# Turning a small accumulation around on TensorE: 32-column tiles with v stationary in place of phi(k) stationary

## The chip, the cores and the metric

The kernel runs on one core of one Trainium2 chip. The metric is the device time of one execution in microseconds (us). Three runs of the kernel before gave 148.71, 149.34 and 149.08 us, so the median is 149.08 us.

## The reference, cut to what matters

One transformer layer with a linear attention and a dense block side by side, over 2048 rows of 448 numbers, 16 heads of 28:

```python
xn  = layernorm(x)                              # 2048 x 448
q, k, v = split_heads(xn @ wqkv)                # 16 heads of 28
pq, pk  = q @ w_phi[h], k @ w_phi[h]
phi_q = concat(softmax(pq), softmax(-pq))       # 56 features per head
phi_k = concat(softmax(pk), softmax(-pk))
kv  = phi_k^T @ v                               # per head 56 x 28, summed over all 2048 rows
z   = sum over rows of phi_k                    # per head 56
num = phi_q @ kv ;  den = phi_q @ z + 1e-6
out = x + merge_heads(num / den) @ wo + silu(xn @ w1) @ w2
```

The change is about `kv` and `z`. All heads together they are 16 small products of 56 x 2048 by 2048 x 29, where a column of ones beside the 28 columns of v gives z.

## The kernel before, in words

The 2048 rows are 16 tiles of 128, in 4 chunks of 4. A tile t of phi(k) lies in `E[:, t % 6, 1, :]`: 128 rows, 16 heads of 64 columns each, 56 used and 8 of zeros. The matching v lies in `vb` as 16 x 29 columns.

Every matmul of the kernel uses half of TensorE's rows. Two matmuls stand side by side, one on partitions 0 to 63 and one on 64 to 127 (`pair`, `tpair`, L437 and L450), and write two different PSUM banks. All stationary operands have 128 columns.

The units of work on TensorE are these. `F1(c, i)` is a block of 14 matmuls of 512 columns for the dense layer's hidden activations of chunk c. `QK(t)` and `V(t)` are 14 matmuls of 448 columns for one tile's q and k, and for v of two tiles. `F2_early(t)` and, for the late tiles, `F2_ph` are 28 matmuls of 448 columns for the dense layer's second product. `KV(t)` adds one tile to `kv`. `U(t)` multiplies phi(q) of two tiles by `kv`. `WO` is the output projection.

`KV(t)` (L731) takes two heads at a time. The stationary operand is a 64-row half of phi(k) with 128 columns (two heads), the moving operand the 58 columns of v of the same two heads. Half of the 128 x 58 result is a product of one head with the other and is never read. That is 8 pairs, 16 matmuls per tile, 256 in the whole. The sums of the two halves of the rows stand in PSUM banks 6 and 7.

`KVZ_fin` (L738) ends the sum: for each of two partition ranges, ScalarE copies bank 6 to `KVt` and VectorE adds bank 7 and writes `KVZ`, in which `U` finds kv with the 56 features on the partitions.

Around this, the order of TensorE's work is the order in which the program text issues it. Everything else is placed by a planner (`_Prog.schedule`) that walks the operations with assumed durations and due times; it fixes the order on ScalarE, VectorE, GpSimd and the DMA queue, and semaphores are set from the data dependencies. In chunk 1 and chunk 2, four `KV` stand one by one between `F1` blocks. In chunk 3, two `KV` follow `V(12)` and two follow `QK(15)`, and the last four stand between the `F1` blocks. So the 16 `KV` are 14 places on TensorE: 12 of one tile and 2 of two tiles. After the last `KV` come `F1(3, 5)`, then `KVZ_fin`'s result is used by `U(0)`, which stands after the first pair of `F1(3, 6)`; `U(8)` stands inside the first half of the late `F2` of tiles 8 and 9, after its fourth step (ft = 3); then `U(2)`.

Of the kernel before, what the change touches and what calls it, by code (L numbers as in the profile page):

```python
# [7 lines left out]
F32 = mybir.dt.float32  # L8
ACTF = mybir.ActivationFunctionType
# [320 lines left out]
def bass_parallel_sum__linear_kernel_hedgehog__dense_activation_silu__prompt_kernel(  # L330
# [10 lines left out]
    S, D, H, DH, FF = 2048, 448, 16, 28, 1792  # L341
    NT = S // 128
# [3 lines left out]
    NCH = S // 512  # L346
# [5 lines left out]
    with es:  # L352
        def sb(name, shape, dt):
            return es.enter_context(nc.sbuf_tensor(name, shape, dt))

        NE, NV, NX, NXC, NYE, NH = 6, 3, 4, 3, 8, 3
# [9 lines left out]
        E = sb("E", [128, NE, 2, 1024], BF16)  # L366
        vb = sb("vb", [128, NV, 2, H * (DH + 1)], BF16)
        xnd = sb("xnd", [128, NX, NS * 128], BF16)
        Ye = sb("Ye", [128, NYE, D], F32)
        KVZ = sb("KVZ", [128, 8, DH + 1], BF16)  # L370
        KVt = sb("KVt", [128, 8, DH + 1], F32)
        BD = sb("BD", [128, NB, 2 * DH], BF16)
        ident = sb("ident", [128, 128], BF16)
        neghalf = sb("neghalf", [128, 1], F32)
# [28 lines left out]
        def bank(b):  # L403
            return psum[:, b * 512:(b + 1) * 512]

        def bank16(b):
            return psum16[:, b * 1024:(b + 1) * 1024]
# [11 lines left out]
        P = _Prog()  # L419
# [14 lines left out]
        def d_dve(n, mode=1):  # L434
            return n * 1.042 / mode + 158.0

        def pair(mms, n, name, dur=None):  # L437
            reads = []
            writes = []
            for (dst, lhsT, rhs, st, sp) in mms:  # L440
                reads += [lhsT, rhs]
                writes.append(dst)

            def fn(e):
                for (dst, lhsT, rhs, st, sp) in mms:
                    ins = e.matmul(dst, lhsT, rhs, start=st, stop=sp, skip_group_check=True)  # L446
                return ins
            return P.op("pe", dur if dur else max(n / 2.4 + 2.5, 27.0), fn, reads=reads, writes=writes, name=name)

        def tpair(trs, n, name):  # L450
            reads = []
            writes = []
            for (dst, src, idn) in trs:
                reads += [src, idn]
                writes.append(dst)

            def fn(e):
                for (dst, src, idn) in trs:
                    ins = e.transpose(dst, src, idn)  # L459
                return ins  # L460
            return P.op("pe", max(n / 2.4 + 2.5, 29.0), fn, reads=reads, writes=writes, name=name)

        def act(dst, src, func, n, table=None, scale=1.0, name="", reads=None, writes=None):
            return P.op("act", d_act(n), lambda e: e.activation(dst, src, func, scale=scale),  # L464
                        reads=reads or [src], writes=writes or [dst], table=table, name=name)

        def dve(fn, dur, reads, writes, name):
            return P.op("dve", dur, fn, reads=reads, writes=writes, name=name)
# [12 lines left out]
        HALF = (LO, HI)  # L481
# [199 lines left out]
        def F1(c, i, mid=None):  # L681
            P.unit = f"F1_{c}_{i}"
            sl = take()
            for s in range(NS):
                pair([(bank(2 * sl + q)[:, 0:512], w1_sb[HALF[q], s, i * 128:(i + 1) * 128],
                       xw(q, c, s, 0, 512), s == 0, s == NS - 1) for q in range(2)], 512, "f1")
                if mid is not None and s == 0:
                    mid()
            F1silu(sl, i, c, 0, 512)
# [40 lines left out]

        def KV(t):  # L731
            P.unit = f"KV{t}"
            for c in range(8):
                pair([(bank(6 + q)[:, c * 58:(c + 1) * 58], E[HALF[q], t % NE, 1, c * 128:(c + 1) * 128],
                       vb[HALF[q], (t // 2) % NV, t % 2, c * 58:(c + 1) * 58], t == 0 and c == 0, t == NT - 1)
                      for q in range(2)], 58, "kv")

        def KVZ_fin():  # L738
            P.unit = "KVZ"
            for q, (p0, p1) in enumerate(((0, 56), (64, 120))):  # L740
                v = [bank(6 + b)[p0:p1, 0:464].rearrange("p (c n) -> p c n", n=58)[:, :, q * 29:(q + 1) * 29] for b in range(2)]
                tmp = KVt[p0:p1]
                act(tmp, v[0], ACTF.Identity, 232, name="kvz_a")
                dst = KVZ[p0:p1]
                dve(lambda e, dst=dst, a=v[1], tmp=tmp: e.tensor_tensor(dst, a, tmp, ALU.add), d_dve(232), [v[1], tmp], [dst], "kvz_d")

        def F2(t, mid=None, at=7):
            c, j = divmod(t, 4)
# [22 lines left out]
            for q in range(2):  # L771
                act(bk[q], xs[q], ACTF.Identity, b - a, name="seed")

        def F2_ph(t, sl, ph, a, b, mid=None, at=3):
            c, j = divmod(t, 4)
            for ft in range(FT):
                P.unit = f"F2_{t + ph}"
                mms = []
                for q in range(2):
                    h = q ^ ph  # L780
                    mms.append((bank(2 * sl + h)[:, a:b], hT[HALF[q], c % NH, ft, (j + h) * 128:(j + h + 1) * 128],
                                w2_sb[HALF[q], ft, a:b], False, False))
                swapped(pair(mms, b - a, "f2"), (2 * sl, 2 * sl + 1), ph)
                if mid is not None and ft == at:
                    mid()

        uc = [0]

        def U(t, sl=3):
            P.unit = f"U{t}"  # L790
            for i, tt in enumerate((t, t + 1)):
                for c in range(8):
                    o0 = i * 232 + c * 29
                    pair([(bank(2 * sl + q)[:, o0:o0 + 29], phT[q * 64:q * 64 + 56, tt, c, :], KVZ[q * 64:q * 64 + 56, c, :], i == 0 and c == 0, True)
                          for q in range(2)], 29, "u", dur=25.0)
            ub = uc[0] % NO
            uc[0] += 1
            Uv = two(sl)[:, :, 0:464].rearrange("p b (c n) -> p b c n", n=29)
            dn = den[:, ub, :].rearrange("p (b c) -> p b c", b=2)
            dve(lambda e: e.tensor_scalar(dn, Uv[:, :, :, DH], EPS_DEN, None, ALU.add), 200, [Uv], [den[:, ub, :]], "den")  # L800
            dve(lambda e: e.reciprocal(rden[:, ub, :], den[:, ub, :]), 360, [den[:, ub, :]], [rden[:, ub, :]], "rden")
            for i in range(2):
                for q in range(2):
                    src = bank(2 * sl + q)[:, i * 232:(i + 1) * 232].rearrange("p (c n) -> p c n", n=29)[:, :, 0:DH]
                    src = src.rearrange("p c (s e) -> p c s e", e=4)
                    r = rden[:, ub, q * 16 + i * 8:q * 16 + (i + 1) * 8]
                    rb = r[:, :, None, None].broadcast_to([128, 8, NS, 4])
                    dst = o_pr[:, ub].rearrange("p (s n) -> p s n", s=NS)[:, :, i * 64:(i + 1) * 64].rearrange("p s (c r e) -> p c r s e", r=2, e=4)[:, :, q]
                    dve(lambda e, dst=dst, src=src, rb=rb: e.tensor_tensor(dst, src, rb, ALU.mult), d_dve(224),  # L809
                        [src, r], [dst], "o")  # L810
            P.dma(lambda e: e.dma_start_transpose(out=oT[:, ub], in_=o_pr[:, ub]), 0, reads=[o_pr[:, ub]],
                  writes=[oT[:, ub]], name="oT_dma", issue=1250.0, fixed=3100.0)
            return ub
# [227 lines left out]

        ub = {}

        def first_u():
            ub[EPAIRS[0]] = U(EPAIRS[0])

        LATE = list(range(8, 16))
        EPAIRS = [0, 2, 4, 6]
        for c in range(NCH):
            if c == NCH - 1:  # L1050
                phase_e(c, F2E[c])
            if c > 0:
                for i in range(FH):
                    F1(c, i, first_u if c == NCH - 1 and i == 6 else None)
                    if i in ((3, 4, 5, 6) if c == 1 else (1, 2, 4, 5) if c == 2 else (1, 2, 3, 4)):
                        kv(1)
                    if c == NCH - 1 and i == 4:
                        KVZ_fin()
            if c < NCH - 1:
                phase_e(c, F2E[c])  # L1060
                if c < NCH - 2:
                    for t in range(4 * c + 8, 4 * c + 12):
                        prep(t)
        def nextu(t, sl=3):
            if sl is None:
                sl = take()
                give(sl)
            ub[t] = U(t, sl)

        sls = {}  # L1070

        def ph0(l, a, b, mid=None):
            sls[l, a] = take()
            seed(l, sls[l, a], a, b)
            F2_ph(l, sls[l, a], 0, a, b, mid)
# [7 lines left out]
            WO_two(l, ub[l], sls[l, 0], 0, D)  # L1083

        M = D // 2
        ph0(8, 0, D, lambda: nextu(8, None))
        nextu(2)
        ph1(8, 0, D)
        ph0(10, 0, D)
# [123 lines left out]
```

## Time and profile before

| | us |
|---|---|
| median of three runs | 149.08 |
| the profiled execution, whole | 148.71 |
| its span (first to last instruction) | 147.0 |
| TensorE matmuls busy | 142.4 (97%) |
| TensorE weight loads busy | 87.8 (60%) |
| VectorE busy | 92.3 (63%) |
| ScalarE busy | 89.0 (61%) |
| GpSimd busy | 76.3 (52%) |

The granted TensorE clock is full from the second of the 40 slices of the span on. A matmul's end is modelled, so the busy times of matmuls that lie side by side overlap; what a unit costs TensorE is read from the time between its first start and the first start of what follows. The difference of 1.7 us between the whole and the span lies outside the profile.

### The profile page before, as it was taken

The page shows a single profiled execution, that of the slowest core. Times are in us where ns is not written, and L with a number is a line of the kernel's source. Part 1 is how long each engine was busy: PE and PEld are TensorE (multiplying, and loading weights), DVE is VectorE, ACT ScalarE, POOL GpSimd, SP SyncE. Part 2 cuts the span into 40 slices and gives each one's busy share as a digit, 9 for nine tenths or more (in the row PEclk, how much of TensorE's full clock was granted, in tenths as well). Part 3 has the DMA queues.
Part 4 walks back from the last instruction along what each step waited for, and adds up shares of the span by engine and source line. Part 5 has one row for each costly group of instructions (what it writes and reads, how often), then busy time and mean ns, then how long its engine had stood idle before and what let it go on. Part 6 is the DMA issues. An engine that isn't in the chain of part 4 may idle for free.

```text
span 147.0 us, 5049 instructions
## 1 busy us (share of the span) xinstructions
PE 142.4 (97%) x2188; PEld 87.8 (60%) x2188; DVE 92.3 (63%) x176; ACT 89.0 (61%) x119; POOL 76.3 (52%) x87
## 2 busy tenths in 40 slices
PE   6999999999999999999999999999999999999992
PEld 2589975555556555555555556655555555557871
DVE  1977469999977496840167997871067254466632
ACT  4248789997767784975987767598593023040401
POOL 3335025059999959899122999999980000000000
PEclk9999999999999999999999999999999999999999
DMA  5997989985930895359870049333663505315473
GB/s 142 389 253 159 329 250 256 78 166 157 164 78 4 159 181 123 90 131 151 173 158 0 0 101 46 71 76 74 85 134 71 121 4 179 75 60 131 127 129 125
DMA packets 44110, 19.11 MB, mean 130 GB/s; under 512 B 37240, under 2 KB 43448, under 8 KB 44088
## 3 DMA queue, kind: packets, MB, share of 16 engines
q1 hardware_dynamic: 43432, 17.87, 57.9%
q10 hardware_dynamic: 656, 0.92, 1.7%
q8 instruction: 17, 0.28, 0.9%
q14 instruction: 5, 0.04, 0.1%
HBM read 8.17 MB, written 1.84 MB: 68 GB/s over the span
## 4 chain that ended last, share of the span: by engine, by line
PE 93%; DMA 3%; DVE 1%; POOL 0%; issue 0%; ACT 0%; SPq 0%; POOLq 0%
PE psum L446 92%; DMA E<-E 3%; PE psum L459 1%; DVE E L809 1%; POOL hT L485 0%; DVE x_sb L843 0%; ACT xT L464 0%; POOL neghalf L484 0%; SPq L1153 0%; POOLq L1198 0%
## 5 line engine op out<-in xcount | busy, mean ns | idle before, releaser
L713 POOL TENSOR_TENSOR E<-E,Rk 128x896 bf16<-128x896 bf16 x32 | 53.3, 1700 | 7.0 <-DVE Rk L708 5.3
L446 PE MATMUL psum<-xT,w_sb 64*128 64x512 bf16 (+2 forms) x522 | 46.8, 324 | 0.3 <-ACT xT L464 0.3
L446 PE MATMUL psum<-w_sb,hT 64*128 64x448 bf16 (+1 forms) x504 | 45.3, 328 | 0.0
L446 PEld LDWEIGHTS psum<-w_sb,hT 64*128 64x128 bf16 x504 | 25.7, 94 | 16.4 <-ACT psum L464 0.2
L706 DVE TENSOR_REDUCE Sk<-E 128x64 f32<-128x1792 bf16 x16 | 31.9, 2004 | 2.9 <-ACT E L464 2.9
L446 PEld LDWEIGHTS psum<-xT,w_sb 64*128 64x128 bf16 x522 | 25.1, 94 | 13.9 <-issue 0.4
L464 ACT ACTIVATE hT<-psum 128x1024 bf16<-128x1024 f32 (+1 forms) x29 | 28.1, 993 | 8.8 <-PE psum L446 8.5
L464 ACT ACTIVATE E<-psum 128x896 bf16<-128x896 f32 x32 | 27.4, 917 | 6.4 <-PE psum L446 5.2
L446 PE MATMUL psum<-wqk,xT 64*128 64x448 bf16 x224 | 23.7, 349 | 0.0
L446 PEld LDWEIGHTS psum<-wqk,xT 64*128 64x128 bf16 x224 | 12.2, 94 | 8.6
L464 ACT ACTIVATE psum<-x_sb 128x448 f32<-128x448 bf16 (+1 forms) x10 | 4.6, 470 | 20.0 <-PE psum L446 19.4
L581 POOL TENSOR_TENSOR rstd<-ve,neghalf 128x1 f32<-128x1 f32 x16 | 9.1, 571 | 7.2 <-DVE ve L579 6.4
L765 POOL TENSOR_TENSOR Ye<-Ye,x_sb 128x448 f32<-128x448 f32 x8 | 8.2, 1037 | 8.8 <-DVE Ye L763 8.8
L446 PE MATMUL psum<-wo_sb,E 64*128 64x448 bf16 (+1 forms) x126 | 11.9, 328 | 0.1
L446 PE MATMUL psum<-wv_sb,xT 64*128 64x448 bf16 x112 | 12.0, 349 | 0.0
L589 DVE TENSOR_SCALAR xnd<-x_sb,mv,rstd 128x896 bf16<-128x896 bf16 x12 | 8.3, 723 | 5.9 <-POOL rstd L581 5.9
L573 DVE BATCH_NORM_STATS2 st<-x_sb 128x6 f32<-128x448 bf16 x16 | 9.5, 605 | 3.3 <-DMA x_sb<-in_A_x_dram 3.3
L763 DVE TENSOR_TENSOR Ye<-psum,Ye 128x448 f32<-128x448 f32 x8 | 5.0, 622 | 10.3 <-ACT Ye L464 10.2
L833 DVE TENSOR_TENSOR x_sb<-psum,Ye 128x448 bf16<-128x448 f32 x8 | 4.8, 607 | 9.7 <-PE psum L446 6.8
L809 DVE TENSOR_TENSOR E<-psum,rden 128x224 bf16<-128x224 f32 x32 | 10.2, 383 | 0.2
L446 PEld LDWEIGHTS psum<-wv_sb,xT 64*128 64x128 bf16 x112 | 5.9, 94 | 4.0
L446 PEld LDWEIGHTS psum<-wo_sb,E 64*128 64x128 bf16 x126 | 5.8, 94 | 4.0 <-DMA E<-E 0.4
(48 smaller groups left out, 100.0 us busy)
## 6 DMA issues: line engine op xcount, KB each, us to landing
w_sb<-in_B_w_dram SPq DMA_DIRECT2D x4, 448.0 KB, 5.8
out_dram<-x_sb SPq DMA_DIRECT2D x7, 224.0 KB, 2.1
w_sb<-in_B_w_dram SPq DMA_DIRECT2D x4, 336.0 KB, 6.7
x_sb<-in_A_x_dram SPq DMA_DIRECT2D x2, 448.0 KB, 4.8
wv_sb<-in_A_wqkv_dram SPq DMA_DIRECT2D x2, 392.0 KB, 5.3
wo_sb<-in_A_wo_dram SPq DMA_DIRECT2D x14, 56.0 KB, 2.3
phT<-in_A_wqkv_dram SPq DMA_DIRECT2D x3, 224.0 KB, 4.6
w_sb<-in_B_w_dram ACTq DMA_DIRECT2D x1, 448.0 KB, 4.5
```

Source lines behind the costliest of these rows:

```text
L446: ins = e.matmul(dst, lhsT, rhs, start=st, stop=sp, skip_group_check=True)
L459: ins = e.transpose(dst, src, idn)
L464: return P.op("act", d_act(n), lambda e: e.activation(dst, src, func, scale=scale), reads=reads or [src], writes=writes or [dst], table=ta ...
L573: P.op("dve", 630, lambda e: e.bn_stats(st6[:, t, :], xs), [xs], [st6[:, t, :]], name="bnst", ordered=od)
L581: P.op("pool", 580, lambda e: e.tensor_tensor(rstd[:, t:t + 1], ve[:, t:t + 1], neghalf[:], ALU.pow), [ve[:, t:t + 1], neghalf[:]], [rstd[ ...
L589: dve(lambda e: e.tensor_scalar(dst, src, mv[:, t, 0:1], rstd[:, t:t + 1], ALU.subtract, ALU.mult), 734, [src, mv[:, t, 0:1], rstd[:, t:t ...
L706: dve(lambda e: e.tensor_reduce(Sk[:, t % 3, :].rearrange("p (h g) -> p h g", g=2), Er, AXL.X, ALU.add), d_dve(1792), [Er], [Sk[:, t % 3, ...
L713: pool(lambda e, Eh=Eh, Rb=Rb: e.tensor_tensor(Eh, Eh, Rb, ALU.mult), 1770, [Eh, Rh], [Eh], "phi%d" % qk)
L763: dve(lambda e: e.tensor_tensor(y, b, y, ALU.add), d_dve(D), [b, y], [y], "ye_d")
L765: pool(lambda e: e.tensor_tensor(y, y, x_sb[:, t, :], ALU.add), 1110, [y, x_sb[:, t, :]], [y], "ye_x")
L809: dve(lambda e, dst=dst, src=src, rb=rb: e.tensor_tensor(dst, src, rb, ALU.mult), d_dve(224), [src, r], [dst], "o")
L833: dve(lambda e, bk=bk, y=y, dst=dst: e.tensor_tensor(dst, bk, y, ALU.add), d_dve(D), [bk, y], [dst], "out")
```

## The change

`KV` is turned around. v is now the stationary operand, one head at a time (64 rows x 29 columns), and phi(k) of that head moves (64 rows x 64 columns). The 29 result rows go to PSUM partitions 0, 32, 64 or 96 and up, so four heads lie in four 32-column tiles of the array, each with both row halves: eight matmuls stand together for four heads, 32 per tile of rows, 512 in the whole. The result is kv transposed, 29 x 64 per head.

`KVZ_fin` becomes one ScalarE copy of 256 columns and one VectorE addition of 256 columns, which writes the sum as bf16 into `KVb`, a part of the buffer `xnd`. A new unit `KVZ_tr` turns it with four TensorE transposes into banks 6 and 7, and one ScalarE and one VectorE copy of 116 columns bring it to `KVZ`.

`KVZ_tr` takes the place of `U(0)` in `F1(3, 6)`. `U(0)` moves into the first half of the late `F2` of tiles 8 and 9, after its second step (ft = 1), and `U(8)` there from after ft = 3 to after ft = 4. On the DMA queue two phi(q) transposes change places with transposes of chunk 3's input, in the middle of the kernel. The order on GpSimd is the same.

```diff
-        KVt = sb("KVt", [128, 8, DH + 1], F32)
+        KVt = sb("KVt", [128, 256], F32)
+        KVb = xnd[:, 0, 0:256]
...
         def KV(t):
             P.unit = f"KV{t}"
-            for c in range(8):
-                pair([(bank(6 + q)[:, c * 58:(c + 1) * 58], E[HALF[q], t % NE, 1, c * 128:(c + 1) * 128],
-                       vb[HALF[q], (t // 2) % NV, t % 2, c * 58:(c + 1) * 58], t == 0 and c == 0, t == NT - 1)
-                      for q in range(2)], 58, "kv")
+            for a in range(4):
+                mms = []
+                for j in range(4):
+                    h = 2 * ((j // 2) * 4 + (a // 2) * 2 + j % 2) + a % 2
+                    for q in range(2):
+                        mms.append((bank(6 + q)[32 * j:32 * j + 29, a * 64:(a + 1) * 64],
+                                    vb[HALF[q], (t // 2) % NV, t % 2, h * 29:(h + 1) * 29],
+                                    E[HALF[q], t % NE, 1, h * 64:(h + 1) * 64], t == 0 and a == 0, t == NT - 1))
+                pair(mms, 64, "kv", dur=40.0)
 
         def KVZ_fin():
             P.unit = "KVZ"
-            for q, (p0, p1) in enumerate(((0, 56), (64, 120))):
-                v = [bank(6 + b)[p0:p1, 0:464].rearrange("p (c n) -> p c n", n=58)[:, :, q * 29:(q + 1) * 29] for b in range(2)]
-                tmp = KVt[p0:p1]
-                act(tmp, v[0], ACTF.Identity, 232, name="kvz_a")
-                dst = KVZ[p0:p1]
-                dve(lambda e, dst=dst, a=v[1], tmp=tmp: e.tensor_tensor(dst, a, tmp, ALU.add), d_dve(232), [v[1], tmp], [dst], "kvz_d")
+            v = [bank(6 + b)[:, 0:256] for b in range(2)]
+            act(KVt[:], v[0], ACTF.Identity, 256, name="kvz_a")
+            dve(lambda e: e.tensor_tensor(KVb, v[1], KVt[:], ALU.add), d_dve(256), [v[1], KVt[:]], [KVb], "kvz_d")
+
+        def KVZ_tr():
+            P.unit = "KVZ"
+            for b in range(2):
+                tpair([(bank16(6 + q)[:, b * 64:(b + 1) * 64], KVb[HALF[q], b * 128:(b + 1) * 128], ident[HALF[q], q * 64:(q + 1) * 64])
+                       for q in range(2)], 64, "kvz_tr")
+            for q in range(2):
+                src = bank16(6 + q)[:, 0:128].rearrange("p (c n) -> p c n", n=32)[:, :, 0:29]
+                dst = KVZ[:, 4 * q:4 * q + 4, :]
+                if q:
+                    dve(lambda e, dst=dst, src=src: e.tensor_copy(dst, src), d_dve(116), [src], [dst], "kvz_e")
+                else:
+                    act(dst, src, ACTF.Identity, 116, name="kvz_e")
...
-                    F1(c, i, first_u if c == NCH - 1 and i == 6 else None)
+                    F1(c, i, KVZ_tr if c == NCH - 1 and i == 6 else None)
...
-        ph0(8, 0, D, lambda: nextu(8, None))
+        ph0(8, 0, D, {1: lambda: nextu(0), 4: lambda: nextu(8, None)})
```

## The prediction

> **What bounds the kernel now.** I read the busy table and the chain that ended last first, since they say which engine's time the change has to shorten.
>
> ```profile
> PE 142.4 (97%) x2188; PEld 87.8 (60%) x2188; DVE 92.3 (63%) x176; ACT 89.0 (61%) x119; POOL 76.3 (52%) x87
> ...
> PE psum L446 92%; DMA E<-E 3%; PE psum L459 1%; DVE E L809 1%; POOL hT L485 0%; DVE x_sb L843 0%; ACT xT L464 0%; POOL neghalf L484 0%; SPq L1153 0%; POOLq L1198 0%
> ```
>
> TensorE is busy 97% of the span and its matmuls are 93% of the chain. Nothing else is above 63%. So time added to or taken from TensorE's queue between 39 us (the first KV) and 106 us (the last) goes to the end almost one for one. The DMA piece of the chain is at 138 to 142 us, behind the last U; nothing of the change lies there, it only slides.
>
> Next the groups of TensorE, with shapes kept apart. The last two columns are busy us and mean ns of one.
>
> ```profile
> L446 PE MATMUL psum<-vb,E 64*128 64x58 bf16 x256 | 6.1, 187 | 0.0
> L446 PE MATMUL psum<-KVZ,phT 56*128 56x29 bf16 x256 | 4.5, 173 | 0.0
> L446 PEld LDWEIGHTS psum<-vb,E 64*128 64x128 bf16 x256 | 6.0, 94 | 2.8
> ```
>
> Every matmul row of this view reads 64\*128 or 56\*128: one shape of the array, half the rows and all 128 columns, from the first matmul to the last. The change brings in a shape that no row here has. A KV matmul is modelled at 187 ns although its 58 columns stream in far less: most of a matmul is a fixed tail that normally lies under the next ones.
>
> What a unit really takes is the distance of starts in TensorE's timeline (start us, then us from first start to last modelled end).
>
> ```profile
> 100.11 0.40 PE L446 MATMUL psum<-vb,E 64*128 64x58 bf16 x16
> 100.34 1.69 PE L446 MATMUL psum<-xT,w_sb 64*128 64x512 bf16 x14
> 101.85 0.40 PE L446 MATMUL psum<-vb,E 64*128 64x58 bf16 x16
> 102.08 1.69 PE L446 MATMUL psum<-xT,w_sb 64*128 64x512 bf16 x14
> ...
> 107.28 0.57 PE L446 MATMUL psum<-KVZ,phT 56*128 56x29 bf16 x32
> 107.69 1.47 PE L446 MATMUL psum<-xT,w_sb 64*128 64x512 bf16 x12
> ```
>
> A KV takes 102.08 - 101.85 = 0.23 us, the double ones 90.02 - 89.56 = 0.46 us. Sixteen are 16 x 0.23 = 3.68 us, 2.5% of the kernel: all that a better KV could ever give. U runs 32 matmuls of 29 columns in 107.69 - 107.28 = 0.41 us, 12.8 ns each.
>
> ```profile
> 11.24 0.37 PE L459 MATMUL psum<-ident,xnd 64*128 64x64 bf16 x14
> 11.45 0.82 PE L446 MATMUL psum<-xT,w_sb 64*128 64x256 bf16 x12
> ```
>
> This row has the moving width of the new KV: 14 transposes of 64 columns, seven pairs in 0.21 us, 30 ns per pair. Two parts of the array stream 64 columns in the time of one.
>
> **The matmuls of KV.** Removed: 16 x 16. Added: 16 x 32, each of 64 columns, eight to a group on eight parts of the array. If all eight run as the two above do, a group is 30 ns, a KV 4 x 30 = 0.12 us, and the gain is 16 x (0.23 - 0.12) = 1.76 us. If each load with its matmul takes its turn as in U, a KV is 32 x 12.8 = 0.41 us, and the loss is 16 x 0.18 = 2.88 us. I take 0.12, since in every paired row two tiles overlap, and keep 0.41 for the range.
>
> **The loads.** There are twice as many, of 29 columns in place of 128. All of TensorE's loads show 92 to 102 ns in steady work and cost nothing beside a matmul stream (the pairs above carry 14 of them in 0.21 us); I put no term on them beyond the two ends just named. [...] No trace here has such a load.
>
> **The changes of shape.** The 16 KV stand in 14 places between blocks of the old shape, so the array changes shape 28 times, and no row shows what one costs. At the lower end it costs nothing, as going from 512 columns to 58 does now (7 pairs of F1 and then KV, no idle time). A gain from changing shape has no reason. At the upper end the next matmul waits until the last one is out: 187 ns less the 29 ns that a KV pair takes now (0.23 / 8), 158 ns. Between them stands the load row: if only the first load cannot be fetched ahead, its 94 ns come into the open. I take the middle of 94 and 158, 126 ns, because a change of shape that costs at all must expose at least the load behind it. That is 28 x 0.126 = 3.53 us; the ends are 0 and 28 x 0.158 = 4.42 us. [...]
>
> **The end of kv.** Four transposes are added, two pairs of 30 ns: 0.06 us on TensorE. Beside it, not on its path:
>
> ```profile
> 105.88 0.74 ACT L464 ACTIVATE KVt<-psum 56x232 f32<-56x232 f32 x2 [1.05 <-PE psum L446]
> 106.34 0.82 DVE L745 TENSOR_TENSOR KVZ<-psum,KVt 56x232 bf16<-56x232 f32 x2 [6.45 <-ACT KVt L464]
> 107.77 1.01 ACT L464 ACTIVATE psum<-x_sb 128x448 f32<-128x448 bf16 x2
> 108.98 0.93 PE L446 MATMUL psum<-w_sb,hT 64*128 64x448 bf16 x8
> 109.78 0.57 PE L446 MATMUL psum<-KVZ,phT 56*128 56x29 bf16 x32
> ```
>
> Two ScalarE copies of 0.37 and two VectorE adds of 0.41 become one of each, some 0.02 us longer for 24 more columns. The sum is ready at about 106.7 instead of 107.16, and the transposes stand at 107.28: no wait. ScalarE wins 0.35, so the two seeds of the late F2 end near 108.43 and the new ScalarE copy of 116 columns (under the 0.37 of 232) near 108.8. U(0) now comes after four matmuls of F2, which itself starts 0.41 - 0.06 earlier: 108.98 - 0.35 + 4 x 0.095 = 109.01. The cover is 0.2 us; gone, it would cost TensorE about as much. I book nothing.
>
> **U(0) and U(8) closer together.** U(0)'s evacuation now takes from its end now (107.69) to the end of its last VectorE op (108.76 + 1.28 = 110.04) 2.35 us. From 109.42 that gives 111.8. U(2) uses the same banks 6 and 7 and stands at 112.08: cover 0.3 us. U(8)'s own evacuation then queues behind it on VectorE and ends near 113.7, U(2)'s near 115.6 instead of 114.86. Their transposing DMAs are first wanted by WO(0) at 117.79 and for tile 8 at 119.52. No stall. The two phi(q) transposes that change places on the DMA queue with input transposes are first read by U, after 107 us; zero.
>
> **The sum.** -1.76 + 3.53 + 0.06 = +1.83 us on the profiled execution: 148.71 becomes 150.54. That execution is the lowest of three; the median stands 0.37 above it, so I predict 150.9 us, with 150.0 to 151.8 as this case's own range (switches of 94 to 158 ns: +0.9 to +2.7).
>
> **The rivals.** Differences of 0.5%, 0.75 us, are about what a measurement of this kernel can tell from no change.
>
> *Faster.* The array is switched for little. For it: no stall between any two forms in the trace, and eight streams side by side are only more of what pairs do. Against it: no row has a second shape. The price that decides is 1.70 / 28 = 61 ns per switch; at 34 ns or less the gain passes 0.75 us. At zero the median is 147.4. Chance 0.30, 147.4 to 148.3.
>
> *No change.* Switches of 34 to 88 ns eat the gain. Chance 0.10, 148.3 to 149.8.
>
> *Much slower.* Eight tiles don't run at once, loads and matmuls take turns: +2.88 + 0.06, and switches of 0 to 4.42 on top, 152.0 to 156.4. For it: U's 12.8 ns each at half the columns, a rate set by something other than streaming. Against it: that may be a floor per half of the array, as two halves at 25.6 ns. Chance 0.20.
>
> *Forecast.* The rest, 0.40. Slower in all 0.60.
>
> The range, 147.4 to 154.2, takes in the faster case whole and the much slower one up to switches of about 80 ns (+2.94 + 2.24 = +5.2); it leaves out about half of that case's 0.20 and a little at the low end.
>
> **What would show it.** In the timeline after, KV rows read 29 to 64 columns; the distance from a KV's first start to the next block's start less 0.12 is the price of its two switches, 0.25 us by the forecast, so 0.37 us per single KV. The double KV are the cleanest: 0.24 + 0.25 = 0.49, and a double less a single is the matmuls of one KV alone, 0.12 by mine, 0.41 by the much slower case. Under 0.18 us per single the faster rival holds. A gap between the seeds and U(0), or an idle TensorE before U(2), would show my zero terms wrong.

## The result, and the profile after

The changed kernel takes 150.88 us (median of four runs, 150.62 to 151.22) where the kernel before, run beside it, takes 149.00 us. The ratio is 1.0127, with a 95% interval of 1.0092 to 1.0161: slower by 1.9 us. The profiled execution took 150.62 us with a span of 148.9, 1.91 us over that of before on both counts.

The busy table and the chain of the kernel after:

```profile
PE 144.3 (97%) x2448; PEld 82.5 (55%) x2448; DVE 92.2 (62%) x176; ACT 88.7 (60%) x119; POOL 76.3 (51%) x87
...
PE psum L447 96%; PE psum L460 1%; POOL hT L486 0%; DVE x_sb L859 0%; ACT xT L465 0%; POOL neghalf L485 0%; POOLq L1211 0%
```

TensorE still carries the chain. The DMA piece at the end of the chain of before is gone, which the prediction did not have. In the groups with shapes kept apart the new shape shows (busy us, mean ns of one, then idle time before and what ended it):

```profile
L447 PE MATMUL psum<-E,vb 64*29 64x64 bf16 x512 | 5.3, 193 | 0.0
L447 PEld LDWEIGHTS psum<-E,vb 64*29 64x29 bf16 x512 | 3.6, 88 | 5.9 <-issue 5.4 <-POOL ve L580 0.4
```

The loads of the new KV stand behind 5.4 us of idle time that nothing in the profile explains ("issue"); before, that group had 2.8 us of idle time and no such note. In the timeline of the kernel before, the loads of a KV start 0.21 us ahead of its first matmul (101.85 - 101.64); in that of the kernel after, loads and matmuls start together (the last two lines).

```profile
101.64 0.50 PEld L446 LDWEIGHTS psum<-vb,E 64*128 64x128 bf16 x16
...
105.61 0.19 PEld L447 LDWEIGHTS psum<-E,vb 64*29 64x29 bf16 x32 [0.42 <-issue]
105.61 0.31 PE L447 MATMUL psum<-E,vb 64*29 64x64 bf16 x32
```

The timeline of TensorE's matmuls shows what this costs.

```profile
89.21 1.49 PE L447 MATMUL psum<-wv_sb,xT 64*128 64x448 bf16 x14
90.62 0.78 PE L447 MATMUL psum<-E,vb 64*29 64x64 bf16 x64
91.33 1.50 PE L447 MATMUL psum<-wqk,xT 64*128 64x448 bf16 x14
...
98.77 3.19 PE L447 MATMUL psum<-xT,w_sb 64*128 64x512 bf16 x28
101.89 0.31 PE L447 MATMUL psum<-E,vb 64*29 64x64 bf16 x32
102.13 1.69 PE L447 MATMUL psum<-xT,w_sb 64*128 64x512 bf16 x14
103.75 0.32 PE L447 MATMUL psum<-E,vb 64*29 64x64 bf16 x32
```

From one single KV to the next, with one F1 between, it was 101.85 - 100.11 = 1.74 us and is 103.75 - 101.89 = 1.86: 0.12 us more. The F1 alone takes 1.51, so a single KV with its edges now costs 0.35 us where it cost 0.23. Part of the price stands ahead of the KV: from the first matmul of the F1 to the first of the KV it is 103.75 - 102.13 = 1.62 instead of 1.51 us.

A double KV with the block before it, V(12), took 90.02 - 88.23 = 1.79 us and takes 91.33 - 89.21 = 2.12, and the block behind it takes another 0.01: 0.34 us more. A double costs 0.81 with its edges, a single 0.35, so the second KV of a double costs 0.46 us, nearly four times what the forecast gave a KV's matmuls. The lines of before:

```profile
88.23 1.50 PE L446 MATMUL psum<-wv_sb,xT 64*128 64x448 bf16 x14
89.56 0.63 PE L446 MATMUL psum<-vb,E 64*128 64x58 bf16 x32
90.02 1.50 PE L446 MATMUL psum<-wqk,xT 64*128 64x448 bf16 x14
...
97.09 3.20 PE L446 MATMUL psum<-xT,w_sb 64*128 64x512 bf16 x28
```

### The profile page after: what moved, and what is told of

Read it like the earlier page. It is cut to its first block, busy times and chain, and to the rows that moved or that the text cites. A ratio compares the mean times of both kernels' runs of the same rounds, so it can differ in the third digit from the quotient of the medians.

```text
span 148.9 us, 5571 instructions
## 1 busy us (share of the span) xinstructions
PE 144.3 (97%) x2448; PEld 82.5 (55%) x2448; DVE 92.2 (62%) x176; ACT 88.7 (60%) x119; POOL 76.3 (51%) x87
## 4 chain that ended last, share of the span: by engine, by line
PE 97%; POOL 0%; issue 0%; DVE 0%; ACT 0%; POOLq 0%
PE psum L447 96%; PE psum L460 1%; POOL hT L486 0%; DVE x_sb L859 0%; ACT xT L465 0%; POOL neghalf L485 0%; POOLq L1211 0%
## 5 line engine op out<-in xcount | busy, mean ns | idle before, releaser
L447 PEld LDWEIGHTS psum<-w_sb,hT 64*128 64x128 bf16 x504 | 24.4, 94 | 17.3
L447 PEld LDWEIGHTS psum<-xT,w_sb 64*128 64x128 bf16 x522 | 23.7, 95 | 15.7 <-issue 0.4
L447 PEld LDWEIGHTS psum<-wqk,xT 64*128 64x128 bf16 x224 | 11.1, 94 | 9.7
L709 DVE RECIPROCAL Rk<-Sk 128x64 f32<-128x64 f32 x16 | 8.2, 533 | 0.1
L465 ACT ACTIVATE vb<-psum 128x896 bf16<-128x896 f32 x8 | 7.4, 924 | 0.9 <-PE psum L447 0.9
```

The source lines that it names most:

```text
L709: dve(lambda e: e.reciprocal(Rk[:, t % 3, :], Sk[:, t % 3, :]), 64 * 6.25 + 155, [Sk[:, t % 3, :]], [Rk[:, t % 3, :]], "Rk")
```

## Experiments

Two theories of the edges were to be told apart. The first: changing the shape of the array costs a fixed time, about 0.11 us each way, whatever is computed. The second: what is lost at the edges is the load of the new operand or its wait. There were two more for the second KV of a double: either instructions do not arrive fast enough once a first stock is used up, or that KV waits for data of its own.

**One pair of the new shape in the old kernel.** KV stays as it was. Behind each of its 14 places one pair is added, into columns of banks 6 and 7 that nobody reads.

```diff
+        def extra(t):
+            pair([(bank(6 + q)[0:29, 464:496], vb[HALF[q], (t // 2) % NV, t % 2, 0:29], E[HALF[q], t % NE, 1, 0:32], False, t == NT - 1)
+                  for q in range(2)], 32, "x")
...
             for _ in range(min(n, len(pend))):
-                KV(pend.pop(0))
+                t = pend.pop(0)
+                KV(t)
+            if t is not None:
+                extra(t)
```

> The kernel before, with one pair of 64x32-shaped matmuls (29 columns of v stationary, 32 columns moving, into unused columns of banks 6 and 7) added behind each of the 14 places of KV; its result is read by nobody and it waits for nothing new. Theory (changing the array's shape costs about 0.11 us each way, whatever is computed): each place gets 0.22 us longer, 14 x 0.22 = 3.1 us and up to 0.3 for the pairs, time about 152.2. Rival (what is lost at the edges of KV is its first load, which waits for a semaphore or is slow, not the shape): the pair alone, 14 x 0.026 = 0.4 us or less, time about 149.4.

Measured: 152.33 us, ratio 1.0178 (1.0139 to 1.0217). TensorE's timeline of this run:

```profile
41.60 0.39 PE L446 MATMUL psum<-vb,E 64*128 64x58 bf16 x16
41.92 0.19 PE L446 MATMUL psum<-E,vb 64*29 64x32 bf16 x2
42.05 1.69 PE L446 MATMUL psum<-xT,w_sb 64*128 64x512 bf16 x14
43.57 0.39 PE L446 MATMUL psum<-vb,E 64*128 64x58 bf16 x16
```

Two matmuls of 32 columns make a place 43.57 - 41.60 = 1.97 us, 0.23 more than 1.74. They start 0.32 us after KV does instead of 0.23, and what follows them comes 0.13 us later. The pair waits for no data that KV before it had not waited for. The 0.23 us holds the pair itself, for which the control below gives 0.03, so the change of shape is 0.20 to 0.23 us per place. Over 14 places that is 3.2 us of TensorE time, as the first theory has it; the 2.65 us by which the medians differ has an interval of 2.1 to 3.2.

**The same with the old shape**, as a control: phi(k) stationary with 128 columns, 32 columns of v moving.

```diff
-            pair([(bank(6 + q)[0:29, 464:496], vb[HALF[q], (t // 2) % NV, t % 2, 0:29], E[HALF[q], t % NE, 1, 0:32], False, t == NT - 1)
+            pair([(bank(6 + q)[:, 464:496], E[HALF[q], t % NE, 1, 0:128], vb[HALF[q], (t // 2) % NV, t % 2, 0:32], False, t == NT - 1)
```

> Control for the first run: the kernel before, with one pair of the old shape (128 columns of phi(k) stationary, 32 columns of v moving) added at the same 14 places, into the same unused columns. Both theories: 14 x 0.026 = 0.36 us, time about 149.4, no idle TensorE around KV.

Measured: ratio 0.9986 (0.9963 to 1.0009), no difference, and a place of 43.87 - 42.10 = 1.77 us, 0.03 over 1.74. That is what a pair as such costs; the 0.026 us expected is two matmuls of U, 2 x 12.8 ns.

```profile
42.10 0.42 PE L446 MATMUL psum<-vb,E 64*128 64x58 bf16 x18
42.36 1.68 PE L446 MATMUL psum<-xT,w_sb 64*128 64x512 bf16 x14
43.87 0.42 PE L446 MATMUL psum<-vb,E 64*128 64x58 bf16 x18
```

**The same with one matmul over all 128 rows.** No column tile, only the other row shape.

```diff
+            pair([(bank(6)[:, 464:496], E[:, t % NE, 1, 0:128], vb[:, (t // 2) % NV, t % 2, 0:32], False, t == NT - 1)], 32, "x")
```

> The kernel before, with one matmul over all 128 rows and 128 columns (32 moving columns) added at the same 14 places. If every change of shape costs about 0.11 us each way: 14 x 0.22 = 3.1 us, time about 152.2. If only column tiles cost: 14 x 0.026 = 0.4 us, time about 149.4.

Measured: 152.28 us, ratio 1.0184 (1.0142 to 1.0227).

```profile
42.68 0.51 PE L446 MATMUL psum<-vb,E 64*128 64x58 bf16 x17
43.12 1.68 PE L446 MATMUL psum<-xT,w_sb 64*128 64x512 bf16 x14
44.65 0.51 PE L446 MATMUL psum<-vb,E 64*128 64x58 bf16 x17
```

The place is again 1.97 us. The price does not belong to column tiles or to v's loads; a full 128 x 128 matmul among half-row ones pays the same 0.23 us. What fills the time inside a change, the array running empty or a load that can't be sent ahead, these runs do not separate.

**KV in groups of four.** In chunks 1 and 2 of the changed kernel the four KV stand in one block.

```diff
-                    if i in ((3, 4, 5, 6) if c == 1 else (1, 2, 4, 5) if c == 2 else (1, 2, 3, 4)):
+                    if c < NCH - 1:
+                        if i == 6:
+                            kv(4)
+                    elif i in (1, 2, 3, 4):
                         kv(1)
```

> The changed kernel, with the four KV of chunk 1 and the four of chunk 2 each in one block behind the last F1 of the chunk: 12 changes of shape fewer. Theory (only about the first 64 instructions of a block come at full pace, one KV; from then on about 4 ns per instruction and 0.46 us per KV, as in the second KV of the doubles): a block takes 0.11 + 0.13 + 3 x 0.46 + 0.11 = 1.73 us where four single ones take 4 x 0.352 = 1.41, so 2 x 0.32 = 0.64 us over the changed kernel, about 151.5. Rival (the second KV of a double waits for its own phi(k) from GpSimd): phi(k) is long ready here, every KV takes 0.13, a block 0.74 us, and the time is 2 x 0.67 = 1.3 us under the changed kernel, about 149.5.

Measured: 151.34 us, ratio 1.0132 (1.0067 to 1.0196) to the kernel before: 12 changes of shape fewer than the changed kernel, and no faster that one could tell. The block of chunk 1 takes 45.72 - 44.27 = 1.45 us by its timeline, that of chunk 2 71.24 - 69.64 = 1.60.

```profile
44.27 1.51 PE L447 MATMUL psum<-E,vb 64*29 64x64 bf16 x128
45.72 1.50 PE L447 MATMUL psum<-wqk,xT 64*128 64x448 bf16 x14
```

With 0.11 ahead and 0.01 behind, as for a single, that is 1.57 and 1.72, where 1.73 was expected. Four singles take 1.41. The rival's 0.74 is excluded. The table by stages, TensorE alone, for the block of chunk 1 (stretch, its length, matmuls busy, loads busy, with counts of those that touch the stretch):

```profile
44.27:44.40 0.13, 0.13 (x34) 0.13 (x33) 1.00 0.00 0
44.40:44.50 0.10, 0.10 (x33) 0.09 (x20) 1.00 0.00 0
44.50:44.87 0.37, 0.37 (x56) 0.37 (x33) 1.00 0.00 0
44.87:45.24 0.37, 0.37 (x49) 0.37 (x40) 1.00 0.00 0
45.24:45.61 0.37, 0.37 (x48) 0.37 (x38) 1.00 0.00 0
```

The first KV's loads and matmuls begin within 0.13 us. In the trace no matmul begins in the next 0.10 us. Then each KV takes 0.37 us: load and matmul alternate, 8.3 ns for the two, 4.1 ns per instruction, but every eighth matmul starts 34 ns after the one before it. Chunk 2's block has two more gaps, in its third and fourth KV, and is 0.15 us longer; what they are stays open.

**The same with half the columns.** Only the first 32 of each head's 64 columns move.

```diff
-                        mms.append((bank(6 + q)[32 * j:32 * j + 29, a * 64:(a + 1) * 64],
+                        mms.append((bank(6 + q)[32 * j:32 * j + 29, a * 64:a * 64 + 32],
...
-                                    E[HALF[q], t % NE, 1, h * 64:(h + 1) * 64], t == 0 and a == 0, t == NT - 1))
+                                    E[HALF[q], t % NE, 1, h * 64:h * 64 + 32], t == 0 and a == 0, t == NT - 1))
```

> The groups of four of the run above with only the first 32 of a head's 64 columns of phi(k) moved; half of kv and z is left out. Theory (from the second KV of a block on, instructions arrive at about 4 ns each): the number of instructions is the same, so the second to fourth KV of a block keep their 0.37 us. Rival (the array's streaming sets the pace): they fall by 4 x 13 = 0.05 us or more, to 0.32 or less.

```profile
44.91 1.49 PE L447 MATMUL psum<-E,vb 64*29 64x32 bf16 x128
46.34 0.93 PE L447 MATMUL psum<-wqk,xT 64*128 64x448 bf16 x8
```

The block of chunk 1 is 46.34 - 44.91 = 1.43 us, against 1.45 with all columns, where the rival asked for 0.05 us less in each of three KV (an estimate from 13 ns for 32 columns, as the seven pairs of an F1 give with 512 columns each: 1.51 / 7 / 16). Half the streaming changes next to nothing: in this block the pace of the later KV goes with the number of instructions, 4.1 ns each, and not with the columns.

**The same with one signal per KV.** The 32 matmuls become one operation, so only the last signals.

```diff
-            for a in range(4):
-                mms = []
+            mms = []
+            for a in range(4):
...
-                pair(mms, 64, "kv", dur=40.0)
+            pair(mms, 64, "kv", dur=160.0)
```

> The groups of four of the run above with the 32 matmuls of a KV as one operation, so that one matmul in 32 signals a semaphore and not one in 8. In the groups the eighth matmul of each eight starts 33 ns after the seventh, the others 8 ns. If the signal costs the 25 ns: second to fourth KV from 0.37 to 0.29, time 2 x 3 x 0.08 = 0.45 us under the groups of four, about 150.8 with a before of 149.6. If it is the array or the load of the last tile: no change.

```profile
44.40 1.28 PE L447 MATMUL psum<-E,vb 64*29 64x64 bf16 x128
45.61 1.50 PE L447 MATMUL psum<-wqk,xT 64*128 64x448 bf16 x14
```

The block is 1.21 us, 0.24 less, 3 x 0.08 as expected; the later KV take 0.29 each. The pause ahead of each eighth matmul was its signal, 26 ns. The time, 150.92 us with a ratio of 1.0114 (1.0022 to 1.0205), agrees but does not separate from the groups of four. Even so, a later KV is 0.29, over the 0.23 of the old shape: at these paces no grouping makes the turned KV win.

**One signal per KV in the kernel before**, to see whether signals cost there.

```diff
-            for c in range(8):
-                pair([(bank(6 + q)[:, c * 58:(c + 1) * 58], E[HALF[q], t % NE, 1, c * 128:(c + 1) * 128],
...
-                      for q in range(2)], 58, "kv")
+            pair([(bank(6 + q)[:, c * 58:(c + 1) * 58], E[HALF[q], t % NE, 1, c * 128:(c + 1) * 128],
...
+                  for c in range(8) for q in range(2)], 58, "kv", dur=216.0)
```

> The kernel before with the 16 matmuls of a KV as one operation, so that one matmul in 16 signals and not every second one; nothing else differs. [...]

Measured: a KV is 0.23 us as it was (102.17 to 102.40 in its timeline), ratio 0.9992 (0.9955 to 1.0029). Signals cost nothing that could be measured there, where 32 instructions take 0.23 us, 7.2 ns each.

**Half of each KV.** Groups of four, but each KV has two groups of eight in place of four, so that the edge of a KV and the 64th instruction fall apart.

```diff
-            for a in range(4):
+            for a in range(2):
```

> The groups of four with only the first two of the four groups of eight in each KV: 32 loads and matmuls per KV in place of 64; half of kv and z is left out. Theory (64 instructions lie ready when a block begins, whatever they belong to): two KV, 32 matmuls, run at 3 to 4 ns each, then the gap of 0.1 us, then 8 ns each. Rival (the gap belongs to the first load of the second tile, which carries a wait): the gap comes after 16 matmuls.

The table by stages again, for the block of chunk 1:

```profile
44.02:44.15 0.13, 0.13 (x34) 0.13 (x33) 1.00 0.00 0
44.15:44.25 0.10, 0.10 (x33) 0.09 (x19) 1.00 0.00 0
44.25:44.44 0.19, 0.19 (x40) 0.19 (x17) 1.00 0.00 0
44.44:44.62 0.18, 0.18 (x31) 0.18 (x21) 1.00 0.00 0
```

The first 0.13 us again holds 33 loads, which are now two KV; then the 0.10 us without a start, then 0.18 per half KV, the 0.37 per KV of before. The load that brings the second tile, and a wait with it, lies among the first 33 and has no gap; in this block no load near the gap carries a wait. The gap follows the count of instructions and not the tile. The same run has single half KV, whose places show the fixed part:

```profile
101.47 0.25 PE L447 MATMUL psum<-E,vb 64*29 64x64 bf16 x16
101.65 1.69 PE L447 MATMUL psum<-xT,w_sb 64*128 64x512 bf16 x14
103.27 0.25 PE L447 MATMUL psum<-E,vb 64*29 64x64 bf16 x16
```

A place is 103.27 - 101.47 = 1.80, less F1's 1.51 it is 0.29. So 16 of the 32 matmuls are 0.35 - 0.29 = 0.06 us and what is left without any is 0.29 - 0.06 = 0.23, the price of the added pair in the first run.

**The doubles of chunk 3 taken apart.**

```diff
             V(t)
-            kv(2)
+            kv(1)
             QK(t + 2)
+            kv(1)
             F2_early(f2[1])
+            kv(1)
             QK(t + 3)
-            kv(2)
+            kv(1)
             V(t + 2)
```

> The changed kernel, with the two double KV of chunk 3 taken apart: the four KV stand one by one between blocks of 448 columns, with four changes of shape more. Theory (the second KV of a double is slow because only about the first 64 instructions of a block lie ready): all four take 0.35 us with their edges, 1.41 together where the two doubles take 2 x 0.81 = 1.62, so 0.2 us less than the changed kernel, about 150.6 against a before of 149.0. Rival (every change of shape adds, nothing else): four more of about 0.11, 0.44 us more, about 151.3.

The ratio of 1.0136 (0.9970 to 1.0303) leaves the time open, and the distances decide. From the start of V(12) to the first F1 behind V(14):

```profile
91.56 1.49 PE L447 MATMUL psum<-wv_sb,xT 64*128 64x448 bf16 x14
...
100.92 2.32 PE L447 MATMUL psum<-xT,w_sb 64*128 64x512 bf16 x20
```

That is 9.36 us, against 98.77 - 89.21 = 9.56 in the changed kernel for the same work: 0.20 less with four changes of shape more. This profiled execution took 153.41 us, but what it lost lies outside the stretch: V(12) starts at 91.56 in place of 89.21, 2.35 us later, and a wait of 0.7 us for a DMA stands at the end. The stretch is still slower than before, where the same stretch is 97.09 - 88.23 = 8.86 us.

**The moved U alone.** The kernel before with U(0) and U(8) at their new places.

```diff
-                    F1(c, i, first_u if c == NCH - 1 and i == 6 else None)
+                    F1(c, i)
...
-        ph0(8, 0, D, lambda: nextu(8, None))
+        ph0(8, 0, D, {1: lambda: nextu(0), 4: lambda: nextu(8, None)})
```

> The kernel before with the other half of the change alone: KV as it was, U(0) moved behind the second step of the late F2 of tiles 8 and 9 and U(8) behind the fifth. Theory (this part costs TensorE nothing): the distances of starts on TensorE are as before, U(0) and U(2) don't wait, and the time is that of before within 0.3 us, which is the size of the wait for the last transposing DMA that comes and goes. Rival (the move is part of what the change cost or gave): TensorE idle before U(0) or U(2), or a time 0.5 us or more away.

Measured: 149.19 us, ratio 0.9973 (0.9953 to 0.9994), so 0.3% faster, about the size that was expected to come and go. TensorE does not stand idle before U(0) or U(2): the 4 and 18 matmuls of F2 ahead of them take 0.38 and 1.70 us, 0.095 each. It is the only version here whose interval lies below the kernel before, by less than one could tell in one run. Why it does is not settled: its own profile has a longer wait at the end than that of before, 0.68 us against 0.28, behind this piece of its chain:

```profile
138.65 4.51 DMA E<-E
```

## Why the prediction held, and which of its steps did not

The forecast was 150.9 us and the measured median 150.88; on the profiled execution +1.83 was forecast and +1.91 came. The mechanism is the forecast one: a small gain of the matmuls, lost to a larger price of the changes of shape. But two terms and one left-out term were off, by some 0.3 us and more, and they cancelled; that the sum came this close is luck.

*The changes of shape* were the right cause. Booked were 28 x 0.126 = 3.53 us. The added pair, the full-row matmul and the half KV each give about 0.23 us per place, so 14 x 0.23 = 3.2 us, 0.115 us each way, between the ends of 94 and 158 ns. The sign that was named for it, the distance from a KV to the next block, shows only half: 102.13 - 101.89 = 0.24 in place of 0.37, as the rest stands ahead of the KV. That a change costs anything stood in no trace of before: the 126 ns was the author's estimate between two ends. The runs show the price, 115 ns, and not what fills it. The full-row matmul shows that here a change of rows costs as much as one of columns, a place of 1.97 us in both runs.

*The matmuls of KV* were booked at 0.12 us for all 16. For the first KV of a block that is what came: 2 x 0.06 = 0.12. For the second KV of the two doubles it is 0.46. So the term is 14 x (0.23 - 0.12) - 2 x (0.46 - 0.23) = 1.54 - 0.46 = 1.08 us of gain, not 1.76. This is the step that failed: the paired transposes, from which the 0.12 us was taken, have 28 instructions in 0.21 us, 7.5 ns each, where the booked KV has 64 in 0.12 us, 1.9 ns each. They could not show how fast the instructions of a longer block come. By the forecast's own test, double less single, 0.46 would have pointed to loads and matmuls that take turns in the array. This would have been nearly the right number with the wrong cause: the first KV of every block runs all 32 loads and matmuls in 0.13 us on the same eight tiles, and the run of half KV puts the break at a count of instructions.

In the runs the gap of 0.10 us comes after 33 loads and 32 matmuls, in whole and in half KV. That the first ones lie ready when a block begins was the author's theory; the runs show the count, the gap and the pace behind it, and not where the instructions wait. A signal cost 26 ns behind the gap: the eighth matmul starts 34 ns after the seventh, the others 8.3 ns apart, and with one signal per KV, nine fewer behind the gap, the block was 0.24 us shorter.

*The loads* had no term, and no trace of before has one of 29 columns. In the kernel after they show 88 ns each, against 94 for those of the old KV, and the 32 of a first KV begin with its matmuls within 0.13 us.

*The end of kv* went nearly as worked out. Four transposes took 0.06 us (109.51 - 109.45), and the covers held:

```profile
110.41 0.25 ACT L465 ACTIVATE KVZ<-psum 128x116 bf16<-128x116 bf16 x1
110.81 0.54 PE L447 MATMUL psum<-w_sb,hT 64*128 64x448 bf16 x4
111.19 0.56 PE L447 MATMUL psum<-KVZ,phT 56*128 56x29 bf16 x32
112.66 1.28 DVE L825 TENSOR_TENSOR E<-psum,rden 128x224 bf16<-128x224 f32 x4
114.27 0.56 PE L447 MATMUL psum<-KVZ,phT 56*128 56x29 bf16 x32
```

KVZ is there at 110.66, 0.5 us ahead of U(0) at 111.19, where 0.2 was worked out; U(0)'s last VectorE op ends at 113.94, 0.33 ahead of U(2) at 114.27, where 0.3 was worked out. A little was won beside it. In the kernel before, the loads of U(8) waited for a ScalarE copy of `hT`:

```profile
109.77 0.47 PEld L446 LDWEIGHTS psum<-KVZ,phT 56*128 56x128 bf16 x32 [0.30 <-ACT hT L464]
```

The eight matmuls ahead of it took 109.78 - 108.98 = 0.80 us where eight take 0.76. At its new place U(8) has no such wait, so 0.04 is won.

*Left out* was the end. The prediction said of the DMA piece there that it only slides. In this execution the last transposing DMA is in time. The 28 matmuls ahead of those that read its result take 144.57 - 143.23 = 1.34 us up to the next start, where before it was 142.67 - 141.05 = 1.62, with a wait in it: 0.28 us won. The first two lines are of the kernel before, the last two of the kernel after:

```profile
141.05 1.50 PE L446 MATMUL psum<-w_sb,hT 64*128 64x224 bf16 x28
142.67 1.51 PE L446 MATMUL psum<-wo_sb,E 64*128 64x224 bf16 x28
...
143.23 1.51 PE L447 MATMUL psum<-w_sb,hT 64*128 64x224 bf16 x28
144.57 1.50 PE L447 MATMUL psum<-wo_sb,E 64*128 64x224 bf16 x28
```

The profiles of other kernels with the same ends show this wait coming and going: none with the added pair, 0.7 us of idle loads with the doubles taken apart. That speaks for chance and not for the change, but with one profile of each kernel it is not shown.

The sum as measured, against before: 12 x 0.12 + 2 x 0.34 + 0.06 - 0.28 - 0.04 = 1.86 us, with 1.91 in the two profiled executions. Without the 0.28 at the end the change costs 2.1 to 2.2 us of TensorE time.

*The rivals.* Faster needed 61 ns per change of shape; it is 115. The much slower case is out for the singles, where the eight tiles run at once and all 32 loads and matmuls begin within 0.13 us; 0.46 us, near its 0.41, shows only in the second KV of a double, and from another cause.

## What to carry to other kernels

Where one engine is the bound, price a new shape of its work by its edges: here one excursion into another array shape cost as much as the whole step that it was to speed up, 0.23 us, and a change of rows cost the same as one of columns, 1.97 us per place in both runs. Count instructions as well as columns: in this kernel, where each such block follows long matmuls, instructions beyond about the first 64 of a block came at 4.1 ns each, pauses for signals apart, with 32 columns (a block of 1.43 us) as with 64 (1.45 us). And read the distance of starts over a whole place, block before included, since here half of the price, 0.11 of 0.23 us, stood ahead of the block that caused it.

## What the runs showed of the hardware that was not expected

Eight tiles ran a load and a matmul of 64 columns each in 30 ns (0.06 us for the two groups of a half KV), the time of a pair on two tiles (0.21 us for seven), and the 32 loads of 29 columns of a first KV (88 ns each in the trace after) began with its matmuls within 0.13 us. After the first 65 instructions of a block no matmul started for 0.10 us (the groups of four and the half KV); then it went on at 4.1 ns per instruction, at 32 columns as at 64 (blocks of 1.43 and 1.45 us), beside the pauses for signals. A matmul that signals cost 26 ns more there (0.37 us per KV with four signals, 0.29 with one) and nothing measurable in the old KV (0.23 us with eight signals and with one). A single 128 x 128 matmul among half-row ones cost the same 0.23 us as a pair in 32-column tiles.
